# Induced-set attention and a gated feed-forward layer: the single chunk of stage 1 joins the shared groups

## The chip, the cores and the metric

The kernel runs on one core of a Trainium2 chip. The metric is the device time of one execution in microseconds (us). A core has five engines that run side by side, each with its own queue of instructions that it takes strictly in order: TensorE (PE in the profile: matrix products; PEld is its loading of weights), VectorE (DVE), ScalarE (ACT), GpSimd (POOL) and SyncE (SP, which here only issues DMAs). They wait for each other through semaphores.

## The reference, cut to what matters

```python
B, N, m, C = 4, 12416, 32, 128          # x: [B, N, C], inducing: [m, C]
def mab(q, kv):
    s = (q @ kv.T) / sqrt(C)
    s = s - s.max(-1, keepdims=True)
    a = exp(s); a /= a.sum(-1, keepdims=True) + 1e-9
    return a @ kv
h = mab(inducing, x)                     # stage 1: 32 summaries of a batch
y = mab(x, h)                            # stage 2: every row looks at the 32 summaries
out = (sigmoid(y @ w_gate) * (y @ w_val)) @ w_out      # 1536 hidden columns
```

## The kernel before

**Tiles.** The 12416 rows of a batch lie over 128 partitions as 97 chunks of 128 rows. 96 of them form six groups of 16 chunks (numbers 0 to 5); one chunk is left over and is a group of its own, `NG` = 6, the single chunk. Stage 1 scores a group (32 summaries by 2048 rows) as a 128x512 tile: four blocks of 32 partitions stand side by side. The single chunk is a 32x128 tile, so it uses 32 partitions and 128 columns.

**The steady loop.** The feed-forward layer runs over 97 blocks of 512 rows and 12 slices of 128 hidden columns. A step t is one or two slices of one block: even steps have two (1024 elements a partition), odd steps one (512). Of step t PE makes `v` and, two steps ahead, `g`; ACT turns `g` into tanh (`gate(t + 2)`, line 1013); DVE multiplies (`product(t)`, line 1026, tile `u`); PE projects `u` back (line 1057) and ACT copies each finished block out (line 1075). `v` and `g` have one set of PSUM banks each, so `v` of step t waits until DVE has read `v` of step t - 2, and `g` of step t + 2 until ACT has read `g` of step t.

**Everything else is hung into this loop by a table.** `at(slot, make)` puts a piece of work behind an even step; a slot is two steps, and with `late=True` the piece comes behind the odd step. The order of every engine's queue is therefore written out by hand. While batch b goes through stage 2 and the feed-forward layer, the tables at the end (`parts`, `turns`, `shared`) place stage 1 of batch b + 1; `o` is the slot at which batch b begins. Batch 0's own stage 1 is done ahead of the loop.

**Stage 1 of batches 1 to 3** has two forms. `plan_stage1` treats one group at a time: PE scores it, DVE takes the maximum of every row straight from PSUM (line 231), ACT writes exp(score - maximum), a transpose follows (a DMA for a whole group; PE and a DVE copy, line 263, for the single chunk), PE sums, ACT keeps the sum (line 294). `plan_shared` gives two groups (batch 1) or four (batches 2 and 3) one common maximum and little DVE work: ACT copies the scores to SBUF (line 341), into room of the previous batch's `xT`, named `place(i)`; POOL makes a running maximum by `rise` (three instructions: difference, clamp, sum; lines 345 to 349), first over whole tiles of 512 columns, then over halves of 256 and 128; DVE reduces the last 128 columns (`low`, line 358); POOL adds the negative maximum to each kept tile in turn (line 366); ACT takes exp of each (line 379); SP transposes it by DMA; PE sums. `plan_combine` joins the parts of a batch, `ns` of them.

**Stage 2** of a group sums the exponentials, inverts the sum and spreads the product four times (`a2n`, line 686) on POOL. The inverse is four POOL instructions (lines 418 to 423); for the one group that is planned with `soon`, group 1 of batch 0, it is one DVE reciprocal (line 675).

**The end.** The last block is the single chunk of all four batches. Its last product is cut in two, and so are the copies out and the DMAs: the first half by ACT and SP, the second by DVE and a DMA from ACT's queue.

Of the kernel before, what the change touches and what calls it, by code (L numbers as in the profile page):

```python
# [17 lines left out]
P = 128  # L18
# [8 lines left out]
def kernel(  # L27
# [138 lines left out]
    own = [[s for s in (arrival if b == 0 else [2, NG, 3, 4, 5]) if s not in SHARED[b]] for b in range(B)]  # L166
# [9 lines left out]
    for q in range(2):  # L176
        nc.vector.memset(nm1s[q][:], NEG)
        nc.vector.memset(hsts[q][:, 1, :], 0.0)
# [17 lines left out]
    def at(slot, make, late=False):  # L196
        plan.setdefault((slot, late), []).append(make)
# [130 lines left out]
    def plan_shared(b, o, takes, tops, least, weighs, sums, holds):  # L328
# [14 lines left out]
        def rise(near, far, w):  # L343
            top, r = place(4)[:, 0:w], place(5)[:, 0:w]
            nc.gpsimd.tensor_tensor(out=r, in0=far, in1=near, op=ALU.subtract)
# [3 lines left out]
            nc.gpsimd.tensor_tensor(out=top, in0=near, in1=r, op=ALU.add)  # L349

        def lift(i):
            rise(place(0) if i == 1 else place(4), place(i), 512)
            if i == len(SHARED[b]) - 1:
                for w in (256, 128):
                    rise(place(4)[:, 0:w], place(4)[:, w : 2 * w], w)

        def low():
# [7 lines left out]
            for i in range(len(SHARED[b])):  # L365
                nc.gpsimd.tensor_scalar(  # L366
                    out=place(i),
                    in0=place(i),
                    scalar1=nm[:, no : no + 1],
                    scalar2=BIG,  # L370
                    op0=ALU.add,
                    op1=ALU.min,
                )
# [19 lines left out]
        for i in range(len(SHARED[b])):  # L393
# [79 lines left out]
    def plan_combine(b, lead, weights, joined, fill):  # L473
# [5 lines left out]
        def least():  # L479
            ml = bp.tile([P, 1], F32, tag="ml")  # L480
            src = nm1[:, 0:1]
            for k in range(1, ns, 2):
# [4 lines left out]
                    scalar2=nm1[:, k + 1 : k + 2],  # L487
# [217 lines left out]
    def plan_stage2(b, c, score, take, weigh, far=None, soon=False, lag=None):  # L705
# [311 lines left out]
    def product(t):  # L1017
# [6 lines left out]
        cuts = [0, 512] if 0 < t < NST - 1 else [0, 256, 512]  # L1024
# [22 lines left out]
    def project(upto, now, room):  # L1047
        while queue and queue[-1][0] < upto and room > 0:
# [7 lines left out]
            for i in range(BC):  # L1056
                nc.tensor.matmul(  # L1057
                    acc[0][(i // 2) % len(acc[0])][:, i, :],
                    st["u"][:, k, ts(i, P)],
                    wo16[:, NI * (j % 2) + j // 2, :],  # L1060
                    start=(j == 0 and i in ((0, 2) if len(acc[0]) > 1 else (0,))),
# [4 lines left out]
            if t == NST - 1:  # L1066
                o32 = op.tile([P, BC, C], F32, tag="o32")
                nc.scalar.mul(out=o32[:, 0:2], in_=acc[0][0][:, 0:2], mul=0.5)
                nc.sync.dma_start(ov0[:, 0, 0:2, :], o32[:, 0:2])
                nc.vector.tensor_scalar_mul(out=o32[:, 2:4], in0=acc[0][1][:, 2:4], scalar1=0.5)  # L1070
                nc.scalar.dma_start(ov0[:, 0, 2:4, :], o32[:, 2:4])
# [11 lines left out]
    for b in range(B):  # L1083
# [18 lines left out]
        if b == 0:  # L1102
            parts = {
                NG: (16, (19, 19, 19)),
# [90 lines left out]
```

## Time and profile before

| | |
|---|---|
| median of 3 runs | 717.17 us (717.15 to 717.35) |
| the profiled execution | 717.35 us, its span 715.6 us |
| DVE busy | 698.0 us, 98% of the span |
| ACT busy | 674.7 us, 94% |
| PE busy | 646.9 us, 90% |
| POOL busy | 453.8 us, 63% |

The profiled execution is the slowest of the three by 0.18 us; the 1.75 us between its time and its span lie outside the span. In timelines the first number is the start in us from the start of the span, the second the length; the brackets at the end of a row give the idle time ahead of it on its engine and what ended it. Rows of one engine overlap a little, since an instruction begins before the one ahead has drained; the price of a short instruction in a queue that is always full is therefore the distance of two starts and not its own length.

### The profile page before, as it was taken

The page shows a single profiled execution, that of the slowest core. Times are in us where ns is not written, and L with a number is a line of the kernel's source. Part 1 is how long each engine was busy: PE and PEld are TensorE (multiplying, and loading weights), DVE is VectorE, ACT ScalarE, POOL GpSimd, SP SyncE. Part 2 cuts the span into 40 slices and gives each one's busy share as a digit, 9 for nine tenths or more (in the row PEclk, how much of TensorE's full clock was granted, in tenths as well). Part 3 has the DMA queues.
Part 4 walks back from the last instruction along what each step waited for, and adds up shares of the span by engine and source line. Part 5 has one row for each costly group of instructions (what it writes and reads, how often), then busy time and mean ns, then how long its engine had stood idle before and what let it go on. Part 6 is the DMA issues. An engine that isn't in the chain of part 4 may idle for free.

```text
span 715.6 us, 21646 instructions
## 1 busy us (share of the span) xinstructions
PE 646.9 (90%) x8478; PEld 392.6 (55%) x8478; DVE 698.0 (98%) x857; ACT 674.7 (94%) x1018; POOL 453.8 (63%) x769
## 2 busy tenths in 40 slices
PE   7899899998999989999998989999989889898887
PEld 4555555555555555655555555555555555555555
DVE  4799999999999999999999999999999999999998
ACT  4699999999999999999999999999999999999996
POOL 4458853888558988678657897587737546535100
PEclk9999999999999999999999999999999999999999
DMA  8979964253583245165485142221232123121211
GB/s 172 172 136 180 158 111 104 75 117 80 119 158 81 65 101 118 56 124 111 90 142 119 55 76 71 52 74 46 62 76 60 46 74 61 45 61 45 67 41 46
DMA packets 116726, 65.21 MB, mean 91 GB/s; under 512 B 99824, under 2 KB 101008, under 8 KB 116624
## 3 DMA queue, kind: packets, MB, share of 16 engines
q1 hardware_dynamic: 111936, 49.81, 31.1%
q0 software_dynamic: 4416, 13.90, 10.8%
q8 instruction: 66, 1.08, 0.7%
q14 instruction: 36, 0.29, 0.1%
q10 hardware_dynamic: 272, 0.13, 0.1%
HBM read 27.80 MB, written 25.43 MB: 74 GB/s over the span
## 4 chain that ended last, share of the span: by engine, by line
DVE 51%; issue 22%; PE 14%; ACT 10%; DMA 2%; DVEq 1%; POOL 0%; ACTq 0%; POOLq 0%
DVE u L1026 49%; ACT t L1013 10%; PE acc_ps L1057 6%; PE v_ps L994 5%; DMA xn<-in_x_dram 2%; DVE nm L231 1%; PE hp_ps L279 1%; DVEq L1026 1%; PE g_ps L994 0%; POOL xn L82 0%; ACT a1T L244 0%; ACT hwt L448 0%; PE s_ps L589 0%; PE w_ps L104 0%; DVE nmx L600 0%
## 5 line engine op out<-in xcount | busy, mean ns | idle before, releaser
L1026 DVE SCALAR_TENSOR_TENSOR u<-t,v_ps 128x512 f16<-128x512 f16 (+1 forms) x778 | 674.6, 943 | 0.9 <-ACT t L1013 0.7
L1013 ACT ACTIVATE t<-g_ps 128x512 f16<-128x512 f32 (+1 forms) x777 | 592.8, 820 | 20.3 <-ACT t L1013 11.7
L994 PE MATMUL v_ps<-a2r,hwt 32*128 32x512 f16 (+1 forms) x1188 | 293.5, 371 | 56.1 <-DVE u L1026 55.2
L1057 PE MATMUL acc_ps<-wo,u 128*128 128x128 f16 x4656 | 327.4, 220 | 0.0
L1057 PEld LDWEIGHTS <-u 128*128 128x128 f16 x4656 | 260.9, 98 | 88.1 <-issue 87.2
L994 PE MATMUL g_ps<-a2r,hwt 32*128 32x512 f16 (+1 forms) x1188 | 296.7, 377 | 0.0
L994 PEld LDWEIGHTS <-hwt 32*128 32x128 f16 x2424 | 92.4, 91 | 185.7 <-issue 140.4
L686 POOL TENSOR_TENSOR a2n<-e,rs 128x2048 f16<-128x2048 f16 (+3 forms) x25 | 86.8, 3474 | 5.1 <-DVE rs L675 3.4
L657 POOL TENSOR_TENSOR sum<-e 128x256 f32<-128x256 f16 (+1 forms) x23 | 15.5, 672 | 93.1 <-ACT e L649 93.1
L418 POOL TENSOR_TENSOR near<-sme,minus 128x16 f32<-128x16 f32 (+1 forms) x22 | 65.2, 2962 | 1.6
L1075 ACT ACTIVATE o<-acc_ps 128x512 f32<-128x512 f32 x96 | 58.2, 607 | 0.0
L633 POOL TENSOR_TENSOR rise<-sc 128x256 f32<-128x256 f32 (+1 forms) x22 | 16.3, 740 | 40.9 <-ACT sc L623 40.9
L634 POOL TENSOR_SCALAR rise<-rise 128x256 f32<-128x256 f32 (+6 forms) x110 | 30.1, 273 | 9.7
L637 POOL TENSOR_TENSOR top<-top,rise 128x128 f32<-128x128 f32 (+3 forms) x88 | 28.3, 321 | 7.3
L657 POOL TENSOR_TENSOR sum<-sum 128x128 f32<-128x128 f32 (+3 forms) x92 | 28.3, 308 | 7.2
L633 POOL TENSOR_TENSOR rise<-top 128x128 f32<-128x128 f32 (+3 forms) x88 | 27.2, 309 | 6.9
L640 POOL TENSOR_TENSOR sc<-sc,top 128x512 f32<-128x512 f32 (+1 forms) x22 | 23.9, 1085 | 1.7
L366 POOL TENSOR_SCALAR xT<-xT,nm 128x512 f32<-128x512 f32 x10 | 19.8, 1992 | 0.3
L589 PEld LDWEIGHTS <-xT 128*128 128x128 f16 x388 | 13.0, 96 | 11.7 <-issue 11.3
L82 POOL DMA_DIRECT2D xn<-in_x_dram x25 | 14.8, 601 | 6.5 <-DMA xn<-in_x_dram 5.6
L589 PE MATMUL s_ps<-hT,xT 128*128 128x32 f16 x388 | 18.1, 178 | 0.1
L637 POOL TENSOR_TENSOR top<-sc,rise 128x256 f32<-128x256 f32 (+1 forms) x22 | 16.2, 738 | 1.8
(155 smaller groups left out, 284.0 us busy)
## 6 DMA issues: line engine op xcount, KB each, us to landing
out_dram<-o SPq DMA_DIRECT2D x96, 256.0 KB, 2.3
xn<-in_x_dram POOLq DMA_DIRECT2D x19, 512.0 KB, 7.6
xn<-in_x_dram POOLq DMA_DIRECT2D x4, 544.0 KB, 5.7
a2r<-a2n SPq DMA_TRANSPOSE x29, 4.4
xn<-in_x_dram POOLq DMA_DIRECT2D x1, 384.0 KB, 14.9
wg<-in_moe_w_gate_dram POOLq DMA_DIRECT2D x1, 384.0 KB, 16.4
wv<-in_moe_w_val_dram POOLq DMA_DIRECT2D x1, 384.0 KB, 16.8
wo<-in_moe_w_out_dram POOLq DMA_DIRECT2D x1, 384.0 KB, 16.2
```

The lines of the kernel that those rows point to most:

```text
L418: nc.gpsimd.tensor_tensor(out=near, in0=x, in1=minus, op=ALU.pow)
L589: nc.tensor.matmul(s2[:, j, :], xT[b][:, c + j, :], hT16[b][:], start=(j == 0), stop=whole and j == j1 - 1, skip_group_check=True,)
L633: nc.gpsimd.tensor_tensor(out=r, in0=far, in1=near, op=ALU.subtract)
L634: nc.gpsimd.tensor_scalar(out=r, in0=r, scalar1=BIG, scalar2=0.0, op0=ALU.min, op1=ALU.max)
L637: nc.gpsimd.tensor_tensor(out=top[:, 0:n, 0:w], in0=near, in1=r, op=ALU.add)
L657: nc.gpsimd.tensor_tensor(out=d[:, 0:n, :], in0=src[:, :, 0:w], in1=src[:, :, w : 2 * w], op=ALU.add)
L686: eng.tensor_tensor(out=a2n[:, 0:n, :, :], in0=e.unsqueeze(2).to_broadcast((P, n, 4, m)), in1=rs.unsqueeze(2).unsqueeze(3).to_broadcast((P ...
L994: st[what + "end"] = nc.tensor.matmul(pt[:, k, col : col + nb * P], hw[b][r : r + 32, j // 2, :], a2r[r : r + 32, o : o + nb, :].rearrange ...
L1013: st["tanh"] = nc.scalar.activation(out=st["t"][:, :, c:e], in_=st["g"][:, :, c:e], func=AF.Tanh, scale=0.5)
L1026: u = nc.vector.scalar_tensor_tensor(out=st["u"][:, :, c:e], in0=st["t"][:, :, c:e], scalar=1.0, in1=st["v"][:, :, c:e], op0=ALU.add, op1= ...
L1057: nc.tensor.matmul(acc[0][(i // 2) % len(acc[0])][:, i, :], st["u"][:, k, ts(i, P)], wo16[:, NI * (j % 2) + j // 2, :], start=(j == 0 and ...
L1075: nc.scalar.mul(out=o32[:], in_=acc[0][0][:], mul=0.5)
```

## The change

Stage 1's single chunk of batches 1 to 3 leaves `plan_stage1` and becomes a fifth (in batch 1 a third) member of `plan_shared`. ACT copies its 32x128 scores to a tile `one` (slot 13 of batch 1's table, slot 9 of the others); POOL takes it into the running maximum with one more `rise` on 32 partitions, behind all others and ahead of `low`; POOL adds the negative maximum to `one` behind the kept tiles; ACT takes its exp (slot 25, or 27); SP transposes it by DMA; PE adds its sum to that of a shared group, so `ns` falls by one. Its DVE maximum, PE transpose, DVE copy and own sum are gone. In batches 2 and 3 the DMA that transposes its chunk of x moves from slot 20 to slot -2. The inverse of the `soon` group goes from DVE to POOL. The last product is cut 384|128 instead of 256|256, and the copies out and DMAs with it.

```diff
-    own = [[s for s in (arrival if b == 0 else [2, NG, 3, 4, 5]) if s not in SHARED[b]] for b in range(B)]
+    own = [[s for s in (arrival if b == 0 else [2, 3, 4, 5]) if s not in SHARED[b]] for b in range(B)]
...
+        def score_one():
+            s1 = s1_score_pe(b, NG, "m")
+            st["one"] = s1p.tile([P, 512], F16, tag="a1T", name="one").bitcast(F32)[0:m, 0:P]
+            nc.scalar.copy(out=st["one"], in_=s1[0:m, 0:P])
+
+        def weigh_one():
+            st["a1T"] = s1p.tile([P, 512], F16, tag="a1T", name="a1T")
+            nc.scalar.activation(out=st["a1T"][0:m, 0:P], in_=st["one"], func=AF.Exp)
+
+        def turn_one():
+            st["a1"] = s1p.tile([P, 4, P], F16, tag="a1", name="a1")
+            nc.sync.dma_start(st["a1"][:, 0, 0:m], st["a1T"][0:m, 0:P], transpose=True)
...
             if i == len(SHARED[b]) - 1:
                 for w in (256, 128):
                     rise(place(4)[:, 0:w], place(4)[:, w : 2 * w], w)
+                rise(place(4)[0:m, 0:P], st["one"], P, m)
...
-            for i in range(len(SHARED[b])):
+            for far in [place(i) for i in range(len(SHARED[b]))] + [st["one"]]:
                 nc.gpsimd.tensor_scalar(
-                    out=place(i),
-                    in0=place(i),
-                    scalar1=nm[:, no : no + 1],
+                    out=far,
+                    in0=far,
+                    scalar1=nm[0 : far.shape[0], no : no + 1],
...
+            if i == with_one and k0:
+                s1_sum_pe(b, NG, st["a1"], st["hp"], 0, 1, False, False)
             s1_sum_pe(b, SHARED[b][i], st[i], st["hp"], k0, k1, i % per == 0, (i + 1) % per == 0)
...
+        at(o + one[0], score_one)
+        at(o + one[1], weigh_one)
+        at(o + one[1] + 1, turn_one)
...
-            rs = (s2_inverse if soon else s2_inverse_pool)(n, st["sme"])
+            rs = s2_inverse_pool(n, st["sme"])
...
-        cuts = [0, 512] if 0 < t < NST - 1 else [0, 256, 512]
+        cuts = [0, 256, 512] if t == 0 else [0, 384, 512] if t == NST - 1 else [0, 512]
...
-                nc.scalar.mul(out=o32[:, 0:2], in_=acc[0][0][:, 0:2], mul=0.5)
-                nc.sync.dma_start(ov0[:, 0, 0:2, :], o32[:, 0:2])
-                nc.vector.tensor_scalar_mul(out=o32[:, 2:4], in0=acc[0][1][:, 2:4], scalar1=0.5)
-                nc.scalar.dma_start(ov0[:, 0, 2:4, :], o32[:, 2:4])
+                nc.scalar.mul(out=o32[:, 0:3], in_=acc[0][0][:, 0:3], mul=0.5)
+                nc.sync.dma_start(ov0[:, 0, 0:3, :], o32[:, 0:3])
+                nc.vector.tensor_scalar_mul(out=o32[:, 3:4], in0=acc[0][1][:, 3:4], scalar1=0.5)
+                nc.scalar.dma_start(ov0[:, 0, 3:4, :], o32[:, 3:4])
...
-                NG: (16, (19, 19, 19)),
...
-            turns = (5, 7, 17, 19, 22, 25, 9)
-            shared = (10, 14), (15,), 19, (26, 30), (33, 42), (34, 43)
+            shared = (10, 14), (15,), 19, (26, 30), (33, 42), (34, 43), (13, 25), 0
...
-            parts = {2: (7, (16, 17, 17)), 3: (11, (18, 19, 19)), NG: (32, (47, 47, 47))}
-            turns = (-14, -5, -3, 2, 0, 8, 20)
-            shared = (-6, 2, 10, 14), (7, 11, 15), 23, (26, 30, 42, 46), (40, 42, 49, 51), (45, 53)
+            parts = {2: (7, (16, 17, 17)), 3: (11, (18, 19, 19))}
+            turns = (-14, -5, -3, 2, 0, 8, -2)
+            shared = (
+                (-6, 2, 10, 14),
+                (7, 11, 15),
+                23,
+                (26, 30, 42, 46),
+                (40, 42, 49, 51),
+                (45, 53),
+                (9, 27),
+                3,
+            )
```

POOL's queue in batch 2, from the inverse of a stage 2 group to the additions of the negative maximum (tile `xT_878` holds the kept scores, `nm_0_137` the negative maximum, `a2n` the spread product of stage 2). Before:

```order
L418 TENSOR_TENSOR near<-sme,minus_133 128x16
L419 TENSOR_TENSOR rs<-sme,near 128x16
L420 TENSOR_SCALAR rs<-rs 128x16
L423 TENSOR_TENSOR rs<-near,rs 128x16
L686 TENSOR_TENSOR a2n<-e,rs 128x2048
L366 TENSOR_SCALAR xT_878<-xT_878,nm_0_137 128x512 x4
L375 COPY nm_0_137<-nm_0_137 128x1
```

and with the change:

```order
L437 TENSOR_TENSOR near<-sme,minus_133 128x16
L438 TENSOR_TENSOR rs<-sme,near 128x16
L439 TENSOR_SCALAR rs<-rs 128x16
L442 TENSOR_TENSOR rs<-near,rs 128x16
L705 TENSOR_TENSOR a2n<-e,rs 128x2048
L380 TENSOR_SCALAR xT_878<-xT_878,nm_0_137 128x512 x4
L380 TENSOR_SCALAR one<-one,nm_0_137 32x128
L389 COPY nm_0_137<-nm_0_137 128x1
```

The addition to `one` stands behind the four additions to the kept tiles. Line 366 has become line 380.

ACT's queue in batch 2 from the exp of the first shared group on (`t` is the tanh of a step). Before:

```order
L1013 ACTIVATE t_5474<-g_ps 128x512
L379 ACTIVATE a1T<-xT_878 128x512
L1013 ACTIVATE t_5498<-g_ps 128x1024
L1013 ACTIVATE t_5508<-g_ps 128x512
L1013 ACTIVATE t_5530<-g_ps 128x1024
L1013 ACTIVATE t_5538<-g_ps 128x512
L1075 ACTIVATE o_5552<-acc_ps 128x512
```

and with the change:

```order
L1032 ACTIVATE t_5487<-g_ps 128x512
L393 ACTIVATE a1T<-xT_878 128x512
L1032 ACTIVATE t_5511<-g_ps 128x1024
L350 ACTIVATE a1T<-one 32x128
L1032 ACTIVATE t_5523<-g_ps 128x512
L1032 ACTIVATE t_5545<-g_ps 128x1024
L1032 ACTIVATE t_5555<-g_ps 128x512
L1094 ACTIVATE o_5569<-acc_ps 128x512
```

The exp of `one` stands one tanh behind the exp of the first shared group, ahead of all tanh that follow. Batch 3 has the same rows.

POOL's queue in batch 1 at the end of the running maximum. Before:

```order
L345 TENSOR_TENSOR xT_87<-xT_87 128x128
L346 TENSOR_SCALAR xT_87<-xT_87 128x128
L349 TENSOR_TENSOR xT_87<-xT_87 128x128
L657 TENSOR_TENSOR sum_1385<-e 128x256
L657 TENSOR_TENSOR sum_1387<-sum_1385 128x128
```

and with the change:

```order
L358 TENSOR_TENSOR xT_87<-xT_87 128x128
L359 TENSOR_SCALAR xT_87<-xT_87 128x128
L362 TENSOR_TENSOR xT_87<-xT_87 128x128
L358 TENSOR_TENSOR xT_87<-one,xT_87 32x128
L359 TENSOR_SCALAR xT_87<-xT_87 32x128
L362 TENSOR_TENSOR xT_87<-xT_87 32x128
L676 TENSOR_TENSOR sum_1387<-e 128x256
L676 TENSOR_TENSOR sum_1389<-sum_1387 128x128
```

Three instructions have come between the last `rise` and stage 2's sums; DVE's reduction in `low` reads what the third writes.

More of the change, by code (lines that the diff above doesn't have):

```diff
@@ L325, in plan_stage1, with plan_shared @@
         at(keep, lambda: s1_sum_keep(b, s, st["hp"]))
-    def plan_shared(b, o, takes, tops, least, weighs, sums, holds):
+    def plan_shared(b, o, takes, tops, least, weighs, sums, holds, one, with_one):
         st = {}
@@ L341, in keep, with rise @@
             nc.scalar.copy(out=place(i), in_=st["s1"][:])
-        def rise(near, far, w):
-            top, r = place(4)[:, 0:w], place(5)[:, 0:w]
+        def score_one():
[8 more added lines that the diff above has]
+            nc.sync.dma_start(st["a1"][:, 0, 0:m], st["a1T"][0:m, 0:P], transpose=True)
+        def rise(near, far, w, R=P):
+            top, r = place(4)[0:R, 0:w], place(5)[0:R, 0:w]
             nc.gpsimd.tensor_tensor(out=r, in0=far, in1=near, op=ALU.subtract)
@@ L1057, in project @@
                 nc.tensor.matmul(
[L1058 removed]
+                    acc[0][i // 3 if len(acc[0]) > 1 else 0][:, i, :],
                     st["u"][:, k, ts(i, P)],
                     wo16[:, NI * (j % 2) + j // 2, :],
[L1061 removed]
+                    start=(j == 0 and i in ((0, 3) if len(acc[0]) > 1 else (0,))),
                     stop=(j == NJ - 1),
```

4 lines of the change are left out of this document (2 added, 2 removed).

## The prediction

> **What bounds the kernel now.** I read the page's busy times first, then the busy times of stretches, then the timelines around each place that the change touches. The stretches that hold the shared work of batches 2 and 3 (columns: length; busy time and instructions of PE, PEld, DVE, ACT, POOL; clock; DMA share; GB/s):
>
> ```profile
> 235.00:250.00 15.00, 13.80 (x188) 8.63 (x189) 14.89 (x19) 14.76 (x23) 13.52 (x17) 1.00 0.19 51
> 250.00:265.00 15.00, 13.15 (x153) 7.67 (x152) 15.00 (x20) 14.84 (x24) 12.75 (x23) 1.00 0.39 82
> ```
>
> DVE never rests, so each DVE instruction taken away is worth its time and each DVE wait costs its full length. ACT is all but full beside it, and POOL has one or two us to spare in 15.
>
> **What is taken from DVE.** Single-chunk maximum, single-chunk copy, the reciprocal, and their price from start to start:
>
> ```profile
> 43.69 0.25 DVE L675 RECIPROCAL rs<-sme 128x16 f32<-128x16 f32 x1
> 43.86 8.77 DVE L1026 SCALAR_TENSOR_TENSOR u<-t,v_ps 128x512 f16<-128x512 f16 x10
> ...
> 64.87 0.15 DVE L263 COPY a<-aT_ps 128x32 f16<-128x32 f16 x1
> 64.95 1.80 DVE L1026 SCALAR_TENSOR_TENSOR u<-t,v_ps 128x512 f16<-128x512 f16 x2
> 66.68 0.27 DVE L358 TENSOR_REDUCE nm<-xT 128x1 f32<-128x128 f32 x1
> 66.87 3.52 DVE L1026 SCALAR_TENSOR_TENSOR u<-t,v_ps 128x512 f16<-128x512 f16 x4
> ```
>
> The reciprocal is worth 43.86 - 43.69 = 0.17 us, a copy 0.08, a 128-column maximum 0.19 (that of `low`, of the same width). Three batches give 3 x 0.27 + 0.17 = 0.98 us, 0.14% of the time. That is less than the 0.2% (1.43 us) that a measurement of this kernel can tell from no change, so what is added decides.
>
> **Batch 1, the wait of `low`.** The rows of POOL behind the second `keep`:
>
> ```profile
> 58.71 1.26 POOL L345 TENSOR_TENSOR xT<-xT 128x512 f32<-128x512 f32 x1 [1.79 <-ACT xT L341]
> ...
> 64.20 0.46 POOL L345 TENSOR_TENSOR xT<-xT 128x128 f32<-128x128 f32 x1
> ...
> 65.12 0.46 POOL L349 TENSOR_TENSOR xT<-xT 128x128 f32<-128x128 f32 x1
> 65.87 0.67 POOL L657 TENSOR_TENSOR sum<-e 128x256 f32<-128x256 f16 x1 [0.30 <-ACT e L649]
> ...
> 68.51 3.97 POOL L366 TENSOR_SCALAR xT<-xT,nm 128x512 f32<-128x512 f32 x2
> ```
>
> The last `rise` ends at 65.58 and `low` starts at 66.68: 1.10 us to spare. One more `rise` of 128 columns lasts from 64.20 to 65.58, 1.38, with the gap ahead of it 1.46. That it covers 32 partitions makes it no shorter as far as the trace tells:
>
> ```profile
> L483 POOL TENSOR_SCALAR ml<-ml,nm 128x1 f32<-128x1 f32 x4 | 1.4, 357 | 0.4
> L456 POOL TENSOR_SCALAR quad<-quad 32x1 f32<-32x1 f32 x3 | 1.1, 350 | 0.3
> L808 POOL TENSOR_SCALAR hpart<-hst,we 128x128 f32<-128x128 f32 x4 | 2.4, 604 | 1.5 <-ACT hst L294 1.4
> ```
>
> (350 against 357 ns for one column.) The inverse that comes to POOL ahead of this, its price in another group, and the DMA behind it:
>
> ```profile
> 44.02 3.61 POOL L686 TENSOR_TENSOR a2n<-e,rs 128x2048 f16<-128x2048 f16 x1 [2.12 <-DVE rs L675]
> ...
> 239.47 2.93 POOL L418 TENSOR_TENSOR near<-sme,minus 128x16 f32<-128x16 f32 x1
> ...
> 243.37 3.61 POOL L686 TENSOR_TENSOR a2n<-e,rs 128x2048 f16<-128x2048 f16 x1
> ```
>
> ```profile
> 47.75 1.93 SPq L697 DMA_TRANSPOSE a2r<-a2n  x1
> ```
>
> ```profile
> a2r<-a2n SPq DMA_TRANSPOSE x29, 4.4
> ```
>
> It costs 243.37 - 239.47 = 3.9 us less the 2.1 that POOL now waits for DVE's reciprocal; the 1.8 left are covered by the 1.79 of waiting for ACT at 58.71. The group's DMA, issued at 47.75 and landing some 4.4 later, comes 1.8 later too, at about 54; its data are first used at slot 15, four slots of 1.73 (below) ahead of `low`, at about 59. ACT's extra copy of `one`, a slot ahead of that `keep`, pushes POOL by some 0.14 (estimate: its 0.46 for 512 columns, by width, and a little). So the maximum stands at 65.58 + 1.46 + 0.14 = 67.2, and `low` starts there instead of at 66.68: 0.5 us lost, though DVE without reciprocal, maximum and copy could be there at 66.24. Bounds: 0 to 0.8. The exp of `one` in batch 1 (slot 25, six slots behind `low`, so about 77) comes after POOL's addition (68.51 + 1.3 + 4.0 + 0.6 = 74.4): no wait.
>
> **Batches 2 and 3, the wait of ACT for `one`.** This is the large term. POOL and ACT around the exp of batch 2, then batch 3:
>
> ```profile
> 236.06 0.45 POOL L349 TENSOR_TENSOR xT<-xT 128x128 f32<-128x128 f32 x1
> 236.83 0.67 POOL L657 TENSOR_TENSOR sum<-e 128x256 f32<-128x256 f16 x1 [0.32 <-ACT e L649]
> ...
> 247.08 7.91 POOL L366 TENSOR_SCALAR xT<-xT,nm 128x512 f32<-128x512 f32 x4
> ...
> 415.17 7.91 POOL L366 TENSOR_SCALAR xT<-xT,nm 128x512 f32<-128x512 f32 x4
> ```
>
> ```profile
> 250.18 0.63 ACT L379 ACTIVATE a1T<-xT 128x512 f16<-128x512 f32 x1
> 250.70 3.06 ACT L1013 ACTIVATE t<-g_ps 128x1024 f16<-128x1024 f32 x4
> ...
> 418.79 3.06 ACT L1013 ACTIVATE t<-g_ps 128x1024 f16<-128x1024 f32 x4
> ```
>
> ```profile
> 244.50 0.28 DVE L358 TENSOR_REDUCE nm<-xT 128x1 f32<-128x128 f32 x1
> 244.69 15.64 DVE L1026 SCALAR_TENSOR_TENSOR u<-t,v_ps 128x512 f16<-128x512 f16 x18
> ```
>
> `low` itself has 8 us to spare here (236.51 against 244.50). But the addition to `one` is the fifth behind four of 2 us. In batch 2 POOL comes to the sums 1.2 us later (a `rise` of 1.46, less the 0.3 of idle ahead of 236.83), so the four end at 247.08 + 1.2 + 7.9 = 256.2; the fifth takes 0.6 (604 ns, the row of 128 columns with one scalar a partition), so `one` is ready at 256.8. ACT comes to its exp one 1024-wide tanh behind 250.70, at about 251.65 (four tanh, two of each width, last 3.06; a wide one some 0.95). It waits 5.2 us, and all tanh behind it wait with it. After the exp (0.25) the next tanh, of an odd step, starts at 257.1 and ends at 257.7.
>
> DVE has 18 products in 15.64 us, 1.73 a slot. By 251.65 it is four slots past 244.69; it does the products whose tanh is there and would start the eleventh at 244.69 + 5 x 1.73 = 253.3. That one waits until 257.75: 4.4 us. PE adds to it, since in its queue the `g` of two steps on, which needs that same tanh, stands ahead of the projections and the next `v`:
>
> ```profile
> 252.35 0.39 PE L994 MATMUL g_ps<-a2r,hwt 32*128 32x512 f16 x1
> 252.67 0.84 PE L1057 MATMUL acc_ps<-wo,u 128*128 128x128 f16 x12
> 253.47 0.39 PE L994 MATMUL v_ps<-a2r,hwt 32*128 32x512 f16 x2
> ```
>
> From that `g` to the next `v` it takes 1.1 us, so `v` stands at 257.78 + 1.1 + 0.45 = 259.35 and two products later DVE is about 1.0 further back: 5.4 us in all for batch 2. In batch 3 POOL had no idle time ahead of the sums, so the whole 1.46 counts: ready at 415.17 + 1.46 + 7.9 + 0.6 = 425.1, ACT there at 419.75, the wait 5.4, the loss 5.7.
>
> **The clock.** In those waits PE has nothing to do from about 252.7 to 257.8, 5.1 us. What the trace shows of such a pause:
>
> ```profile
> 1.45 1.03 PE L104 MATMUL w_ps<-xT 128*128 128x512 f16 x2 [1.45 <-DVE xT L99]
> 21.26 0.60 PE L104 MATMUL w_ps<-xT 128*128 128x512 f16 x2 [0.67 <-DVE xT L829]
> 710.22 1.84 PE L1057 MATMUL acc_ps<-wo,u 128*128 128x128 f16 x24
> 715.00:715.50 0.50, 0.00 (x0) 0.00 (x0) 0.00 (x0) 0.00 (x0) 0.00 (x0) 0.52 0.00 0
> ```
>
> The last product ends at 712.06, and from 715.0 on the granted clock is about one half, 3 us later; two equal 512-column products take 1.03 us at the start and 0.60 in the steady state. So I expect half clock when PE comes back. The 1.1 us to the next `v` become about 2.0, and the projections (0.8 us a slot, then about 1.6) make a slot longer than DVE's 1.73 until the clock is back: 1.4 us a batch (bounds 0 and 3). The Trainium skill, page "TensorE: Matmul & The Clock Gate", section "What's actually happening", says that the clock halves after an idle window of about 3.4 us that runs freely, and is whole again after a busy one. Taken strictly, a pause of 5.1 us holds a whole window in half the cases, and the sum would be 1.4 lower; the trace speaks against so strict a reading, since its clock fell 3 us after the last product.
>
> **The rest.** What leaves DVE behind the waits of batches 2 and 3 still counts: -2 x 0.27 = -0.54. ACT's exchange of an exp from PSUM and a copy of a sum for a copy and an exp is even. The DMA transposes of `one` and of the moved chunk join SP's queue; they are used 8 slots later or more, which covers them, and what queues behind them on SP waits at most for their issue. In batch 1 one more use of the four `a1` buffers holds the transpose of group 4 on SP from slot 32 to 34; it is used at slot 45, and behind it stand stores of finished blocks, which have four buffers. POOL's later work shifts by 2 us while everything else shifts by 5. The end:
>
> ```profile
> 711.88 0.38 ACT L1068 ACTIVATE o<-acc_ps 128x256 f32<-128x256 f32 x1 [2.28 <-PE acc_ps L1057]
> 712.10 0.42 DVE L1070 TENSOR_SCALAR o<-acc_ps 128x256 f32<-128x256 f32 x1 [0.38 <-PE acc_ps L1057]
> 712.55 0.42 ACTq L1071 DMA_DIRECT2D out_dram<-o  x1
> ```
>
> DVE's copy gets about 0.13 shorter, ACT's starts 0.2 later and lasts 0.1 longer, and ACT issues the last DMA only behind it, at about 712.6 again: +0.1 (bounds -0.2 and +0.3).
>
> **Sum.** 717.35 (the profiled execution) + 0.5 + 5.4 + 5.7 - 0.54 + 0.1 = 728.5 us without a loss of clock, and 2 x 1.4 more with it: 731.3. The median of the runs lies 0.18 below that execution, so I say 731.0 us, 1.9% slower.
>
> **Rivals.**
> - The waits come, the clock stays: 728.3. For it: the pause is only 2 us longer than the time after which the clock fell, and where the clock's windows lie in another run isn't known. Chance 0.25. One wait with and one without, 729.7, I count to the likeliest.
> - Worse: ACT, at 14.84 of 15 us, doesn't make up what PE's slow restart costs, or the clock stays low longer: another 1.5 a batch, 734. Chance 0.12.
> - The other side: no wait at `one`. Were the addition to `one` done ahead of ACT's 251.65, only the 0.98 us and batch 1's 0.5 would count; with `low` on time too, the whole gain by the rows' own lengths is 3 x (0.27 + 0.15) + 0.25 = 1.5, so 715.7. It decides at 5.2 us: POOL would have to give `one` the place ahead of the four tiles, worth 7.9. The order of POOL's queue has it behind them. Chance 0.04 for faster by over 0.2%, 0.04 for the same, near 716.7.
> - Only one of the two batches waits so: about 724. Both have the same order and the same spare time within 0.3 us; 0.05.
>
> That leaves 0.5 for 731.0. The range 727.0 to 734.5 takes in the clock that stays and most of the worse case. Slower by over 0.2%: 0.92, within: 0.04, faster: 0.04.
>
> **What would show it.** In the new profile: ACT idle for about 5 us ahead of the exp of `one` (line 350) twice, put down to POOL's line 380 and none in batch 1; DVE idle some 4.4 us and more ahead of `u` there, and 1 us ahead of `low` in batch 1; a granted clock under 1 in the two stretches. I am wrong if ACT's exp of `one` finds its input ready, or if the clock's fall costs much more or nothing.

## The result and the profile after

The changed kernel takes 736.17 us (median of four runs, 734.79 to 737.48) against 717.16 us (717.12 to 717.35): 1.0264 times as long, with a 95% interval of 1.0242 to 1.0287. The profiled execution took 737.01 us, its span is 735.2 us, 19.6 us more than before.

DVE's three maxima `low` and the last projections cut both spans into pieces that can be set side by side. `low` starts in the changed kernel at the first three times below; in the kernel before it starts at 66.68, 244.50 and, for batch 3, at the time of the last row:

```profile
70.60 0.28 DVE L372 TENSOR_REDUCE nm<-xT 128x1 f32<-128x128 f32 x1
248.32 0.28 DVE L372 TENSOR_REDUCE nm<-xT 128x1 f32<-128x128 f32 x1
423.72 0.28 DVE L372 TENSOR_REDUCE nm<-xT 128x1 f32<-128x128 f32 x1
412.59 0.28 DVE L358 TENSOR_REDUCE nm<-xT 128x1 f32<-128x128 f32 x1
```

| piece, us | before | after | more |
|---|---|---|---|
| start to `low` of batch 1 | 66.68 | 70.60 | 3.9 |
| to `low` of batch 2 | 177.82 | 177.72 | -0.1 |
| to `low` of batch 3 | 168.09 | 175.40 | 7.3 |
| to the last projections | 297.63 | 304.96 | 7.3 |
| to the end of the span | 5.38 | 6.52 | 1.1 |

The two differences of 7.3 us, from `low` of batch 2 to the last projections, hold the waits of batches 2 and 3, which the prediction had. The first and the last difference it had not, or at a fraction of their size.

**What waits.** The waits of the changed kernel (total us, times, longest), and DVE's products on its page:

```profile
PE g_ps L1013 <- ACT t L1032: 10.6, 3, 5.2
ACT a1T L350 <- POOL one L380: 10.1, 2, 5.1
```

```profile
L1045 DVE SCALAR_TENSOR_TENSOR u<-t,v_ps 128x512 f16<-128x512 f16 (+1 forms) x778 | 675.7, 943 | 18.9 <-PE g_ps L1013 9.4
```

DVE's 778 products are as long as before (675.7 us against 674.6); the idle time ahead of them grew from 0.9 to 18.9 us. ACT waits for `one` twice, 5.05 us each time.

**Batches 2 and 3.** POOL, ACT, PE and DVE around the exp of `one` of batch 2, then ACT and DVE of batch 3:

```profile
252.23 7.91 POOL L380 TENSOR_SCALAR xT<-xT,nm 128x512 f32<-128x512 f32 x4
260.12 0.70 POOL L380 TENSOR_SCALAR one<-one,nm 32x128 f32<-32x128 f32 x1
260.85 0.31 ACT L350 ACTIVATE a1T<-one 32x128 f16<-32x128 f32 x1 [5.05 <-POOL one L380]
261.69 0.58 PE L1013 MATMUL g_ps<-a2r,hwt 32*128 32x512 f16 x1 [5.16 <-ACT t L1032]
261.67 0.69 DVE L1045 SCALAR_TENSOR_TENSOR u<-t,v_ps 128x512 f16<-128x512 f16 x1 [4.17 <-ACT t L1032]
264.26 1.82 DVE L1045 SCALAR_TENSOR_TENSOR u<-t,v_ps 128x1024 f16<-128x1024 f16 x2 [1.90 <-PE g_ps L1013]
266.62 1.82 DVE L1045 SCALAR_TENSOR_TENSOR u<-t,v_ps 128x1024 f16<-128x1024 f16 x2 [0.54 <-PE g_ps L1013]
268.76 3.55 DVE L1045 SCALAR_TENSOR_TENSOR u<-t,v_ps 128x1024 f16<-128x1024 f16 x4 [0.32 <-PE g_ps L1013]
```

```profile
436.28 0.31 ACT L350 ACTIVATE a1T<-one 32x128 f16<-32x128 f32 x1 [5.05 <-POOL one L380]
437.10 0.69 DVE L1045 SCALAR_TENSOR_TENSOR u<-t,v_ps 128x512 f16<-128x512 f16 x1 [4.17 <-ACT t L1032]
439.69 1.82 DVE L1045 SCALAR_TENSOR_TENSOR u<-t,v_ps 128x1024 f16<-128x1024 f16 x2 [1.90 <-PE g_ps L1013]
```

ACT's wait of 5.05 us costs DVE 4.17 us and then, behind PE, 1.90 + 0.54 + 0.32: 6.9 us in batch 2.

**Batch 1.** The spread of the group whose inverse moved (POOL), SP's DMAs behind it, and the score of the single chunk:

```profile
45.78 3.61 POOL L705 TENSOR_TENSOR a2n<-e,rs 128x2048 f16<-128x2048 f16 x1
49.42 1.85 SPq L716 DMA_TRANSPOSE a2r<-a2n  x1
51.31 1.07 SPq L1096 DMA_DIRECT2D out_dram<-o  x1
52.43 1.13 SPq L91 DMA_TRANSPOSE xT<-xn  x1
56.57 0.22 PE L219 MATMUL s_ps<-xT,indT 128*32 128x128 f16 x1 [1.87 <-DMA xT<-xn]
57.43 0.69 DVE L1045 SCALAR_TENSOR_TENSOR u<-t,v_ps 128x512 f16<-128x512 f16 x1 [1.46 <-PE g_ps L1013]
59.32 1.82 DVE L1045 SCALAR_TENSOR_TENSOR u<-t,v_ps 128x1024 f16<-128x1024 f16 x2 [1.20 <-PE g_ps L1013]
62.34 3.75 DVE L1045 SCALAR_TENSOR_TENSOR u<-t,v_ps 128x1024 f16<-128x1024 f16 x4 [1.20 <-PE g_ps L1013]
```

The spread ends 1.76 us later than before (it began at 44.02), so the group's transpose is issued at 49.42 instead of 47.75. The transpose at 52.43 is the single chunk's own `xT`; it stands behind it in SP's queue. Its issue and its time from issue to landing (the last number) in the kernel before, and then that time in the changed kernel:

```profile
50.83 1.14 SPq L91 DMA_TRANSPOSE xT<-xn  x1
xT<-xn SPq DMA_TRANSPOSE x1, 2.2
xT<-xn SPq DMA_TRANSPOSE x1, 4.1
```

So the chunk lands at about 53.0 before and at about 56.5 now: 1.6 us of this are the later issue, and 1.9 us a slower landing. The change also moved the chunk's score from slot 16 to slot 13, which PE reaches before the data have landed: 1.87 us of PE waiting, and DVE loses 1.46 + 1.20 + 1.20 = 3.9 us.

**The clock.** The granted clock (the column that reads 0.50) in stretches of the changed kernel, with the columns of such rows as in the prediction:

```profile
56.70:63.50 6.80, 6.80 (x52) 3.81 (x52) 3.67 (x5) 4.06 (x7) 3.84 (x6) 0.50 0.79 140
258.10:268.30 10.20, 6.61 (x49) 3.94 (x48) 4.19 (x5) 5.91 (x10) 8.94 (x20) 0.50 0.08 27
435.60:442.40 6.80, 5.28 (x38) 2.80 (x38) 2.85 (x4) 4.58 (x8) 5.71 (x16) 0.50 0.12 42
```

It fell three times, with each of the three pauses of PE, for 6.8, 10.2 and 6.8 us. In batch 1 it fell just after a pause of only 1.9 us; in batches 2 and 3 it fell within the pause of 5.2 us (in batch 2 at 258.1, while PE waited from 256.5 to 261.7).

**The end.** The last projections and the last DMA of the changed kernel, then SP's closing waits in the last 2.5 us of the span, for the changed kernel and for the one before:

```profile
728.68 1.78 PE L1076 MATMUL acc_ps<-wo,u 128*128 128x128 f16 x24
730.93 0.40 SPq L1088 DMA_DIRECT2D out_dram<-o  x1
```

```profile
L1217 SPq EVENT_SEMAPHORE  x10: 17/28/28, 733.2 to 735.1; - x10
```

```profile
L1190 SPq EVENT_SEMAPHORE  x5: 17/28/28, 714.2 to 715.5; - x5
```

From the start of the last projections to the last DMA it takes 2.25 us (before: 712.55 - 710.22 = 2.33), so the cut cost nothing up to there. The 1.1 us lie behind that: SP runs through ten semaphore instructions in the last 2.5 us, where it had five left before.

### The profile page after: what moved, and what is told of

Same layout as the page of the kernel before. It is cut to its first block, busy times and chain, and to the rows that moved or that the text cites. A ratio compares the mean times of both kernels' runs of the same rounds, so it can differ in the third digit from the quotient of the medians.

```text
span 735.2 us, 21657 instructions
## 1 busy us (share of the span) xinstructions
PE 655.3 (89%) x8475; PEld 396.7 (54%) x8475; DVE 698.4 (95%) x850; ACT 676.0 (92%) x1018; POOL 461.1 (63%) x783
## 4 chain that ended last, share of the span: by engine, by line
DVE 42%; issue 18%; PE 18%; ACT 10%; POOL 8%; DMA 2%; DVEq 1%; SPq 0%; ACTq 0%; POOLq 0%
DVE u L1045 41%; ACT t L1032 9%; PE acc_ps L1076 8%; PE v_ps L1013 6%; POOL xT L380 2%; DMA xn<-in_x_dram 2%; POOL xT L358 1%; POOL xT L362 1%; POOL a2n L705 1%; PE hp_ps L279 1%; POOL near L437 1%; DVE nm L231 1%; PE g_ps L1013 1%; POOL xT L359 1%; DVEq L1045 1%
## 5 line engine op out<-in xcount | busy, mean ns | idle before, releaser
L1045 DVE SCALAR_TENSOR_TENSOR u<-t,v_ps 128x512 f16<-128x512 f16 (+1 forms) x778 | 675.7, 943 | 18.9 <-PE g_ps L1013 9.4
L1076 PE MATMUL acc_ps<-wo,u 128*128 128x128 f16 x4656 | 332.1, 222 | 0.2
L1076 PEld LDWEIGHTS <-u 128*128 128x128 f16 x4656 | 265.2, 99 | 102.9 <-issue 102.0
L437 POOL TENSOR_TENSOR near<-sme,minus 128x16 f32<-128x16 f32 (+1 forms) x23 | 68.1, 2961 | 1.7
```

The costliest lines, as they stand in the source:

```text
L437: nc.gpsimd.tensor_tensor(out=near, in0=x, in1=minus, op=ALU.pow)
L1045: u = nc.vector.scalar_tensor_tensor(out=st["u"][:, :, c:e], in0=st["t"][:, :, c:e], scalar=1.0, in1=st["v"][:, :, c:e], op0=ALU.add, op1= ...
L1076: nc.tensor.matmul(acc[0][i // 3 if len(acc[0]) > 1 else 0][:, i, :], st["u"][:, k, ts(i, P)], wo16[:, NI * (j % 2) + j // 2, :], start=(j ...
```

## The experiments

My theory after the two traces: four causes, each with its own term. (1) ACT's wait for `one` in batches 2 and 3; (2) in batch 1 the single chunk's `xT`, late behind the delayed transpose, at a score moved earlier; (3) half clock after each pause of PE; (4) something at the end. The rivals were that batch 1's loss is the plain price of POOL's extra `rise`, that PE's slow return is its order and not its clock, and that the end is the price of the 384|128 cut.

### The exp of `one` seven slots later

```diff
-                (9, 27),
+                (9, 34),
```

> The exp of `one` in batches 2 and 3 moves from slot 27 to slot 34, 12 us later, so that POOL's addition to `one` is long done. If the two waits of ACT for it cost what the two traces differ by there (7.3 us in batch 2, 6.9 in batch 3), the time is 736.2 - 14.2 = 722.0 us, ACT no longer waits for POOL's line 380, and the clock falls only once, in batch 1. Rival: a wait of some other work that came later with POOL takes its place (POOL still does one more rise and addition, 2 us, ahead of the kept tiles' exps), then 724 to 730 and another releaser in the waits.

Measured: 722.45 us, 1.0073 times the kernel before (1.0056 to 1.0090), 13.7 us less than the changed kernel. ACT no longer waits for `one`; ACT's waits for POOL in batches 2 and 3 that are left, and PE's at the chunk's score in batch 1:

```profile
ACT e L668 <- POOL sc L659: 0.5, 2, 0.3
ACT a1T L393 <- POOL xT L380: 0.4, 2, 0.2
```

```profile
56.47 0.22 PE L219 MATMUL s_ps<-xT,indT 128*32 128x128 f16 x1 [1.59 <-DMA xT<-xn]
```

In the profiled execution batches 2 and 3 take 6.7 and 6.6 us less than in the changed kernel, so the waits cost nearly all that the two traces differed by. Two small ones came up behind them: POOL's extra two us a batch make the exp of the first kept tile and one group's exp of stage 2 wait 0.2 and 0.3 us, so batches 2 and 3 are still 0.6 and 0.7 us longer than in the kernel before. In batch 1 the wait of 1.59 us is there, but the clock did not fall in this execution, and `low` starts at 68.61: 1.9 us late, not 3.9.

### The addition to `one` ahead of the kept tiles

```diff
-            for far in [place(i) for i in range(len(SHARED[b]))] + [st["one"]]:
+            for far in [st["one"]] + [place(i) for i in range(len(SHARED[b]))]:
```

> POOL adds the maximum to `one` ahead of the kept tiles instead of behind them; the exp of `one` stays at slot 27. This is the point on which the prediction's rival of the other side hung. `one` is ready 7 us before ACT comes, so ACT does not wait for it; but each kept tile is ready 0.7 us later, and with the exp of `one` at slot 34 ACT already waited 0.20 us for the first of them. So ACT waits some 0.9 us there in batches 2 and 3: 722.4 + 2 x 0.7 = 723.8 us. Rival: ACT makes up those 0.7 us, then 722.4.

Measured: 724.29 us (722.11 to 726.43), 1.0099 times (1.0080 to 1.0118). ACT's waits for POOL in batches 2 and 3:

```profile
ACT a1T L393 <- POOL xT L380: 1.7, 2, 0.9
```

The wait for `one` is gone and one of 0.9 us for the first kept tile stands in its place, as expected. It cuts PE's work twice for a moment, in batch 2 as follows and in batch 3 alike (0.61 and 0.27 us):

```profile
256.57 0.39 PE L1013 MATMUL g_ps<-a2r,hwt 32*128 32x512 f16 x2 [0.57 <-ACT t L1032]
257.24 0.58 PE L1013 MATMUL g_ps<-a2r,hwt 32*128 32x512 f16 x1 [0.27 <-ACT t L1032]
```

In batch 2 the clock fell here, at 257.25 and for 6.8 us (the second row's 0.58 us is already half clock); in batch 3 it did not. Batch 2 is 2.9 us longer than in the kernel before, batch 3 1.2. This profiled execution, at 726.43 us, is the slowest of the four. This was the point on which the prediction's rival of the other side hung: with this one order changed, the change costs 7 us and not 19.

### The exp of `one` two slots later

```diff
-                (9, 27),
+                (9, 29),
```

> The exp of `one` in batches 2 and 3 two slots later, at 29: ACT's wait falls from 5.05 us to about 5.05 - 3.46 = 1.6 us in each, DVE's first wait to about 0.7 (it had 0.9 to spare before) and PE's pause to about 1.7 us. If the clock does not fall after so short a pause, what remains of a wait is 0.7 us for the tanh and 0.9 for the g behind it: 722.4 + 2 x 1.6 = 725.6 us. If it falls, as in batch 1 after 1.9 us, 1.5 to 2 us more a batch: 728.6 to 729.6.

Measured: 726.71 us (726.13 to 729.05), 1.0139 times (1.0125 to 1.0153), between the two forecasts. DVE behind the wait of batch 2, where the clock fell at once, and of batch 3, where it fell 2 us later and for half as long:

```profile
261.53 0.69 DVE L1045 SCALAR_TENSOR_TENSOR u<-t,v_ps 128x512 f16<-128x512 f16 x1 [0.71 <-ACT t L1032]
264.12 1.82 DVE L1045 SCALAR_TENSOR_TENSOR u<-t,v_ps 128x1024 f16<-128x1024 f16 x2 [1.90 <-PE g_ps L1013]
...
434.95 1.82 DVE L1045 SCALAR_TENSOR_TENSOR u<-t,v_ps 128x1024 f16<-128x1024 f16 x2 [0.86 <-PE g_ps L1013]
```

ACT waits 1.61 us, DVE 0.71, as worked out from the 0.9 us that it had to spare. PE's pause was 1.44 us in both. What PE adds first is 1.90 us at half clock and 0.86 at full clock: when a short pause brings the fall, and so what it costs, differs from place to place in one execution.

### The reciprocal back on DVE

```diff
-            rs = s2_inverse_pool(n, st["sme"])
+            rs = (s2_inverse if soon else s2_inverse_pool)(n, st["sme"])
```

> Only the one reciprocal goes back to DVE; everything else stays as changed. Theory: in batch 1 GpSimd's inverse makes the group's spread 1.75 us later, SP issues that group's DMA transpose later and the single chunk's behind it, and PE waits 1.9 us for the chunk at slot 13 and comes back at half clock. Then with the reciprocal on DVE the chunk's transpose is issued at about 50.8 us and not 52.4, PE waits 0.3 us at most, the clock does not fall in batch 1, `low` of batch 1 starts at 67.0 to 67.4 us instead of 70.6, and the time is 736.2 - 3.4 = 732.8 us. Rival: what batch 1 lost is the price of POOL's one more rise and of ACT's copy; then `low` stays near 70.6 and the time at 736.

Measured: 733.03 us, 1.0218 times (1.0203 to 1.0233), 3.1 us less than the changed kernel. SP's transpose of the chunk, its score, and `low`:

```profile
51.17 1.14 SPq L91 DMA_TRANSPOSE xT<-xn  x1
54.69 0.23 PE L219 MATMUL s_ps<-xT,indT 128*32 128x128 f16 x1
67.00 0.29 DVE L372 TENSOR_REDUCE nm<-xT 128x1 f32<-128x128 f32 x1 [0.57 <-POOL xT L362]
```

With the transpose issued 1.26 us earlier and landing 2.2 us after its issue, as in the kernel before, PE does not wait, and `low` starts 0.3 us later than in the kernel before, behind a wait of 0.57 us for POOL. That is the real price of the extra `rise` and of ACT's copy in batch 1.

### The score of the chunk at slot 15

```diff
-            shared = (10, 14), (15,), 19, (26, 30), (33, 42), (34, 43), (13, 25), 0
+            shared = (10, 14), (15,), 19, (26, 30), (33, 42), (34, 43), (15, 25), 0
```

> The inverse stays on GpSimd, but the single chunk of batch 1 is scored at slot 15 instead of 13, 3.5 us later. Theory: the chunk's transpose lands at about 56.5 us, slot 15 comes at about 58, so PE does not wait, the clock does not fall there, and the time is 732.8 us, as with the reciprocal on DVE. Rival: POOL's later spread itself holds something else up; then the time stays at 735 to 736.

Measured: 733.08 us, 1.0229 times (1.0211 to 1.0247). The score waits 0.38 us for ACT and no longer for a DMA; behind it `low`:

```profile
61.10 0.22 PE L219 MATMUL s_ps<-xT,indT 128*32 128x128 f16 x1 [0.38 <-ACT xT L341]
69.64 0.29 DVE L372 TENSOR_REDUCE nm<-xT 128x1 f32<-128x128 f32 x1 [0.45 <-POOL xT L362]
```

The profiled execution, at 735.78 us the slowest of the four, began the steady loop 2.4 us late (first product at 33.52 against 31.11; its clock fell once at about 19 us). Without that, `low` is 0.55 us later than in the kernel before. So batch 1's loss takes both moves: the inverse to GpSimd and the score to an earlier slot. Either one undone leaves 0.3 to 0.55 us of it.

### The kernel before with only the reciprocal moved

```diff
-            rs = (s2_inverse if soon else s2_inverse_pool)(n, st["sme"])
+            rs = s2_inverse_pool(n, st["sme"])
```

> The kernel before with only the one reciprocal moved to GpSimd. There the single chunk is scored at slot 16, at about 60 us, and its transpose, 1.7 us later than before, lands at about 56.5. Theory: no wait follows, DVE wins 0.17 us: 717.1 us, the same. Rival: POOL's later spread holds something up by itself; then 718 to 720.

Measured: 717.28 us against 717.29, 1.0004 times (0.9995 to 1.0013). By itself the move costs nothing, as the score stands at slot 16 there; nor does its 0.17 us of DVE time show. The chunk's transpose, issued at 52.55, takes 3.9 us to land here too. The slow landing thus goes with the moved inverse and not with the moved score; why the chunk then lands more slowly, no run here shows.

### PE kept busy in the pause: 15 and 23 matmuls

```diff
+    FILLS = [2 * (first_step[(b, 0)] // 2 + 27) + 3 for b in (1, 2)]
...
+        if t in FILLS:
+            f_ps = ps.tile([P, 4, P], F32, tag="m", name="f_ps")
+            for _ in range(15):
+                nc.tensor.matmul(f_ps[:], wo16[:, 0, :], wo16[:, 0:4, :], start=True, stop=True)
         gate_fill(t + 2)
```

> 15 matmuls of 512 columns that nobody reads, some 0.3 us each, stand in PE's queue just ahead of the g that waits for the tanh behind the exp of `one`, in batches 2 and 3: PE is busy in the pause, and ACT waits as before. If the half clock after the pause is a loss of its own, of about 1.9 us a batch by the rows behind the pause (DVE's waits for g of 1.90, 0.54 and 0.32 us, of which 0.8 would remain), the time is 736.2 - 3.8 = 732.4 us, and the granted clock stays 1.0 at 258 and 435 us. With 1.4 a batch, as in the prediction: 733.4. Rival: PE's order alone makes those waits, then 736.

Measured: 734.79 us (733.52 to 735.77), 1.0243 times (1.0228 to 1.0259). The matmuls took 0.227 us each and not 0.3:

```profile
255.10 3.41 PE L1046 MATMUL f_ps<-wo 128*128 128x512 f16 x15
260.38 0.37 PE L1013 MATMUL g_ps<-a2r,hwt 32*128 32x512 f16 x1 [1.87 <-ACT t L1032]
```

```profile
262.42:265.84 3.42, 3.42 (x34) 2.28 (x32) 3.01 (x4) 2.81 (x5) 2.64 (x10) 0.50 0.21 79
```

A pause of 1.87 us was left, and the clock still fell, 2 us after PE was back, and for 3.4 us, so this run did not price it. With `range(23)` the pause is filled:

> 23 unread matmuls instead of 15: at 0.227 us each they last 5.2 us and fill the pause of PE to within 0.1 us. If any pause of some 1.8 us is enough for the clock to fall, as 15 matmuls left it and as batch 1 has it, then here the clock stays 1.0 at 255 to 275 us and 430 to 445 us, DVE waits 4.2 + 0.9 us a batch and not 7.1, and the time is 736.2 - 2 x 1.7 = 732.8 us. Rival: half clock comes from something else about the wait; then the fall is there again and the time at 734 to 736.

Measured: 733.62 us (731.38 to 733.82), 1.0220 times (1.0207 to 1.0234).

```profile
256.73 5.14 PE L1046 MATMUL f_ps<-wo 128*128 128x512 f16 x23
```

```profile
263.49 7.01 DVE L1051 SCALAR_TENSOR_TENSOR u<-t,v_ps 128x1024 f16<-128x1024 f16 x8 [0.85 <-PE g_ps L1013]
```

```profile
262.00:266.00 4.00, 3.58 (x43) 2.14 (x43) 3.15 (x4) 3.90 (x6) 3.33 (x9) 1.00 0.19 68
```

The clock stays whole, and DVE's losses behind the wait shrink from 1.90 + 0.54 + 0.32 us to 0.85. Between the `low`s, batch 2 takes 173.31 us instead of 175.40, and from there to the last projections it is 303.26 instead of 304.96: half clock was worth 2.1 and 1.7 us. The span of the profiled execution is 3.6 us shorter than the changed kernel's: these 3.8 us and some 2.1 of batch 1, where the clock held this time, less 2.4 by which the steady loop began late (its clock fell for one 3.4 us period at 20 us, ahead of the loop).

### The kernel before with only the end cut 384|128

```diff
-        cuts = [0, 512] if 0 < t < NST - 1 else [0, 256, 512]
+        cuts = [0, 256, 512] if t == 0 else [0, 384, 512] if t == NST - 1 else [0, 512]
...
-                nc.scalar.mul(out=o32[:, 0:2], in_=acc[0][0][:, 0:2], mul=0.5)
+                nc.scalar.mul(out=o32[:, 0:3], in_=acc[0][0][:, 0:3], mul=0.5)
```

> The kernel before with only the last product, its copies and its DMAs cut 384|128 instead of 256|256. The prediction gave it +0.1 us (-0.2 to +0.3). By the changed kernel's trace, where the span ends 6.5 us after the last projections begin and not 5.4, it is +1.1: 718.4 us. Rival: that 1.1 us comes from elsewhere; then 717.3.

Measured: 717.38 us against 717.29, 1.0009 times (0.9999 to 1.0018). The 0.1 us that the prediction gave the cut is what the medians show, though the interval takes in no change; from the last projections to the end of the span it is 5.47 us, 5.38 in the kernel before. The 1.1 us of the changed kernel come from elsewhere: the expectation's rival, not its forecast.

### The kernel before with three more DMAs on SP

```diff
+    spare = const.tile([m, 3, 4], F32, tag="spare")
+    def more_dma():
+        for k in range(3):
+            nc.sync.dma_start(spare[:, k, :], inducing[:, 0:4])
+    at(70, more_dma)
```

> The kernel before with three small DMAs more on SP's queue, at slot 70, that nobody reads. In the changed kernel SP issues three DMA transposes more, and the span ends 6.1 to 6.5 us after the last projections begin instead of 5.4, with the end cut either way. SP's closing waits, one for each of its DMA semaphores in a fixed order, stand after the landing of the last store there, and most of them ahead of it in the kernel before. If three more DMAs turn that order, the span here grows by the same 0.6 to 0.8 us: 718.0 us. Rival: the later end comes from something else in the changed kernel; then 717.3.

Measured: 718.38 us against 717.20, 1.0019 times (1.0010 to 1.0028). The last projections and SP's closing instructions in the last 2.5 us:

```profile
710.36 1.84 PE L1057 MATMUL acc_ps<-wo,u 128*128 128x128 f16 x24
```

```profile
L1197 SPq EVENT_SEMAPHORE  x10: 17/28/28, 714.3 to 716.4; - x10
```

Three DMAs that nobody reads, issued 560 us ahead of the end, lengthen it from 5.4 to 6.1 us: ten closing instructions run from the landing of SP's last store on (issued at 712.43, landing 1.9 us later) instead of five. The built programs say why: SP closes with waits for eight DMA semaphores, always in the order 0 to 7, and the DMAs that SP and ACT issue use these eight in turn. The two last stores have numbers 5 and 6 in the kernel before, so most of the list is done by then; they have 0 and 1 in the changed kernel and in this run, so the whole list stands behind them. This is 0.76 us of the changed kernel's 1.1. Some 0.4 us more were lost between 500 us and the last projections; the cause is open.

### The four causes taken away

```diff
-            rs = s2_inverse_pool(n, st["sme"])
+            rs = (s2_inverse if soon else s2_inverse_pool)(n, st["sme"])
...
-            plan_stage2(b, groups[s][0], k, k + 2, k + (14 if more else 10), lag=lag)
+            plan_stage2(b, groups[s][0], k, k + 2, k + ((15 if lag else 14) if more else 10), lag=lag)
...
-            shared = (10, 14), (15,), 19, (26, 30), (33, 42), (34, 43), (13, 25), 0
+            shared = (10, 14), (15,), 20, (26, 30), (33, 42), (34, 43), (13, 25), 0
...
-                (26, 30, 42, 46),
+                (27, 31, 42, 46),
...
-                (9, 27),
+                (9, 34),
```

with the end cut 256|256 again.

> The changed kernel with the four causes taken away: the exp of `one` in batches 2 and 3 at slot 34, the reciprocal on DVE, the end 256|256, and the three small waits for POOL (0.6 us at `low` in batch 1; 0.20 and 0.27 us of ACT in batches 2 and 3) met by putting `low` of batch 1, the exps of the first two kept tiles and one group's exp of stage 2 a slot later. If these are all that the change lost, what is left is DVE's gain of 3 x 0.27 = 0.8 us: 716.5 us. Rival: POOL, later by two us a batch, or ACT makes DVE wait at other places; then 717 to 718.

Measured: 718.33 us against 717.29, 1.0015 times (1.0006 to 1.0024). The steady part is level with the kernel before (the last projections begin at 710.43 us against 710.22), and the end is 6.1 us, 0.7 more, though it is cut as before. So the 0.7 us of SP's closing waits are most of what it loses. DVE's gain of 0.8 us does not show; no wait of DVE of 0.2 us or more is left in the steady part, and where the gain went is open.

### Eight DMAs more, and the exps a slot later again

```diff
-            plan_stage2(b, groups[s][0], k, k + 2, k + ((15 if lag else 14) if more else 10), lag=lag)
+            plan_stage2(b, groups[s][0], k, k + 2, k + ((16 if lag else 14) if more else 10), lag=lag)
...
-                (27, 31, 42, 46),
+                (28, 32, 43, 47),
...
+        for k in range(5):
+            nc.sync.dma_start(spare[:, k, :], inducing[:, 0:4])
```

These are the differences from the run before this one; its other changes stay.

> As b3_best, but with five small DMAs more on SP's queue, so that with the three transposes there are eight more than before, and with the exps of the kept tiles and of the one group of stage 2 one slot later again. If eight semaphores are used in turn, the end is as in the kernel before (5.4 us from the last projections to the end, not 6.1), worth 0.6 us, and the two small waits of batches 2 and 3, 0.16 us each, are gone: 718.3 - 0.6 - 0.6 = 717.1 us, about DVE's gain below the kernel before at best. Rival: the end stays at 6.1 us; then 717.7 or more.

Measured: 739.01 us, 1.0306 times (1.0292 to 1.0320). One slot too many: the inverse of the group's sum fell behind another group's maximum in POOL's queue, its spread came 12.7 us later than in the kernel before (284.19 instead of 271.46), and PE waits for its transpose in batch 2 as shown, and 5.43 us in batch 3:

```profile
295.71 0.60 PE L1013 MATMUL g_ps<-a2r,hwt 32*128 32x512 f16 x2 [9.48 <-DMA a2r<-a2n]
```

The end, though, is as expected: 5.4 us, with most of the closing instructions ahead of the landing.

```profile
L1224 SPq EVENT_SEMAPHORE  x6: 17/28/28, 734.7 to 737.2; - x6
```

With eight more DMAs than in the kernel before the last two stores have semaphores 5 and 6 again. No version with the single chunk in the shared groups came out ahead of the kernel before.

## Why the prediction was wrong, point by point

It forecast 731.0 us with 734.5 as its upper end; 736.2 was measured. The sign, the large term and its mechanism were right; one term was missing and two were too small.

- **ACT's wait for `one`, 5.2 and 5.4 us; DVE's loss 5.4 and 5.7.** Right. ACT waited 5.05 us in both. With the clock held whole by 23 matmuls, batch 2 was 5.2 us longer than in the kernel before and batch 3 5.6, after the 0.27 us that leave DVE in each: the forecast says 5.1 and 5.4. Moving the exp to a later slot takes off 13.7 us at once.
- **Batch 1, 0.5 us (0 to 0.8).** Here the prediction failed, at the step that ends with the group's DMA: 1.8 us later, its data first used at slot 15, so no wait. That is so, and harmless. But the next transpose in SP's queue is the single chunk's own, and the change had moved its score from slot 16 to slot 13; the prediction gave this wait nothing. Its later remark, that transposes are used eight slots later or more, speaks of those of `one` and of the moved chunk in batches 2 and 3; the chunk of batch 1 is transposed at slot 9 as before and now used four slots on. It was issued 1.6 us later and took 4.1 us to land instead of 2.2; with the later issue alone it would have landed at 52.43 + 2.2 = 54.6 (an estimate), about when PE comes to it (54.69 in the run with the reciprocal on DVE). PE's wait was 1.6 to 2.0 us in the six profiled executions that have it. Where the clock held, in two, `low` came 1.9 us late; with half clock behind the wait 2.6 to 4.0, 3.9 in the changed kernel. The two runs without that wait agree with the term as it was worked out: 0.3 and 0.55 us.
- **The clock, 1.4 us a batch (0 to 3).** The mechanism was right, the size too small, though within its bounds: 2.1 and 1.7 us, by the difference to the run with the filled pause. A third fall, some 2 us, came with batch 1's wait. One of the rows that the term rests on does not bear it out: where the two products at 1.45 us take 1.03 us, the granted clock of that trace reads 1.00, so by this column they show no half clock.
- **The end, +0.1 us.** Right for what it described: the cut alone costs 0.1 us or nothing. Missed was that three more DMAs on SP change which of its closing waits the last stores release: 0.76 us. The remaining 0.3 us of the 1.1 were not told apart.
- **POOL's lateness.** The prediction let it vanish, since all else shifts by 5 us. It does vanish behind these waits. With the waits removed it is the next thing that is late, 0.6 us in batch 2 and 0.7 in batch 3.

Summed: 3.9 for PE's wait in batch 1 and its clock, 5.2 + 2.1, 5.6 + 1.7, 1.1 at the end, which is 19.6, the difference of the spans. Batch 1's miss of 3.4 us is the largest; without it the time would have been inside the range, as it was in the two runs that took that wait away, 733.0 and 733.1. The rival "worse", 734, was nearest in number but put its extra time into batches 2 and 3, where the clock cost only 0.7 and 0.3 us more than forecast.

## What to carry to other kernels

When an operation that feeds a DMA gets later, walk down that DMA's queue behind it, and compare each entry with the slot at which it is used in the changed kernel, not in the old one: two moves that do no harm alone, one of a producer and one of a consumer, met in SP's queue and cost 3.9 us. Where an engine waits in a full pipeline, add PE's clock to the price of every pause, even one under 2 us. An in-order engine that adds a constant to several tiles serves them in the written order; put first the one whose reader comes first.

## What the runs showed of the hardware

- **The clock falls with short pauses, on a raster.** In the profiled executions every fall in the steady loop that also ended there lasted 3.4, 6.8, 10.2 or, in the run with eight more DMAs, 13.7 us. In the changed kernel the three falls begin at 56.70, 258.09 and 435.58 us, 59 and 52 steps of 3.413 us apart. Of ten pauses of PE of 1.4 to 2.0 us eight brought a fall, some of them up to 2 us after PE was back; pauses of 1.59 and 1.64 us brought none. Two pauses of 0.57 and 0.27 us close together brought one, two of 0.61 and 0.27 us did not. What decides is not shown. The Trainium skill, page "TensorE: Matmul & The Clock Gate", section "What's actually happening", gives a free-running window of 3413 ns and the half clock after at least one idle window. The lengths and the raster agree with that window; the idle window does not agree, since the clock fell after a pause of 1.87 us.
- **At half clock PE sets the pace.** Behind the waits DVE lost 1.90 + 0.54 + 0.32 us at half clock and 0.85 at full clock. The twelve projections of a slot then last 1.46 us instead of 0.84, PE's other products 0.61 instead of 0.39, and a slot of PE takes 2.36 us (from 262.20 to 264.56), longer than DVE's 1.73 us.
- **The number of DMAs on a queue shows at the end.** Three more, far from the end, cost 0.76 us there, and eight more cost nothing there, since the eight semaphores that SP waits for at the end, in a fixed order, are used in turn.
- **The transpose that was issued later also landed more slowly.** The single chunk's of batch 1 took 2.2 us from issue to landing in the six profiled executions with the reciprocal on DVE, and 3.6 to 4.2 us in the eight with the inverse on POOL, where it was issued some 1.6 us later. The cause is open.
